# Attention and mixture-of-experts kernel: products copied out between two exponentials, one table step and three place matrices moved from GpSimd to ScalarE, and another order in the last slot

## The chip, the cores and the metric

One core of a Trainium2 chip runs one program. It has five engines with an instruction queue each, worked through in order: TensorE (PE, matrix products), VectorE (DVE), ScalarE (ACT), GpSimd (POOL) and SyncE (SP, here for DMA issue). The metric is the device time of one execution in microseconds (us); lower is better. Times of this kernel differ by about 0.2% between runs.

## The reference

```python
def _attn_ref(q, k, v):                     # each 8 x 8 heads x 576 x 64
    ...                                     # rotary embedding of q and k
    scores = scale * np.matmul(q_rot, k_rot.transpose(0, 1, 3, 2))
    scores = scores - np.max(scores, axis=-1, keepdims=True)
    attn = np.exp(scores)
    attn = attn / (np.sum(attn, axis=-1, keepdims=True) + 1e-09)
    return np.matmul(attn, v).astype(np.float32)

def _moe_ref(x, w_gate, w_output_gate, w1, w2):   # x: 4608 x 512, 8 experts, 1024 wide
    logits = x @ w_gate
    e_idx = np.argmax(logits, axis=1)
    ...                                     # gate_w: softmax at e_idx; eom: sigmoid(x @ w_output_gate)
    for e in range(E):
        mask = e_idx == e
        h = np.maximum(x[mask] @ w1[e], 0.0)
        out[mask] = gate_w[mask, None] * eom[mask, e, None] * (h @ w2[e])
```

Attention runs first; its output, with heads and channels brought together, is the x of the experts. Each token goes to one expert.

## The kernel before

The program has two stages. **Attention** takes 32 pairs of heads (8 batches of 4 pairs), one after another, up to about 482 us. A pair has nine units of 128 rows of scores (the two heads' last 64 rows share unit 4), taken in five steps: units 0 and 1, 2 and 3, 4, 5 and 6, 7 and 8. **The experts** take 23 slots of up to 256 tokens of one expert, and in them TensorE sets the pace.

A pair goes through the engines so: TensorE computes a unit's scores into the tile `sc` (L504, twelve matmuls for two units); VectorE copies them to `pm` and takes the row maximum in one instruction (L513, "peak"); ScalarE does the exponential in place with the row sum (L520, "exp"); VectorE transposes `pm` into `pt` (L528 two units in one instruction, L525 one unit). One pair later TensorE multiplies `pt` with the values into `acc` (L550, in four pieces av0 to av3). Then `den0` adds 1e-9 to the row sums (L531, POOL), `den1` takes reciprocals (L534, DVE), `den2` copies one column (L537, ACT), `evict` copies `acc` to `ac` in three instructions (L557 to L559, ACT), `back` turns `ac` round into `acc` again (L565, PE), and `divide` writes the pair's output to `xb` (L577, DVE). Only one `acc` exists, so a pair's first product waits for the `divide` of the pair before it. `pm` has two buffers of two units each (PM).

Ahead of that, POOL rotates a coming pair's q and k (two multiplications L455, one addition L459 and one subtraction L468); ScalarE rounds the result to the type that TensorE takes (`kq`, L465) and copies the last rows' block (`bd`, L475).

After the fourth pair of a batch, `place` finds each token's expert and its row in the experts' lists, spread over the pairs of the next batch as steps s0 to s22: small POOL operations, and at the end five "ones" matrices `ro` (L728 and L729, ACT) and five place matrices `pl` (L738, POOL: where a column's number equals `lo`, the token's number `tok`, else 0), which TensorE multiplies into a list (s20, L746). That list is copied as `lc` (L752, ACT) and added to `lists` (L755, POOL). For the last batch this work is VectorE's and comes behind attention.

The order is written by hand. EVENTS names for each part of a pair an offset in units and a sub-step k; `at` files it there, and `step` issues for each group of units scores, peaks, transposes (TURNS says which units are turned at which step; step 0's entry belongs to the pair before), exps, and then all parts that are filed there, by group and k. ROWS and PLACES do the same for `ro` and `pl`. A framework adds the semaphores; nothing is reordered.

In the experts, a slot's `second` (L1163) does the second layer: four parts of 12 matmuls, the two halves `py_0` and `py_1` of the slot (128 tokens each) taking turns. `store` scales the halves (L1172 on ACT, L1174 on DVE) and scatters the rows to the output by an indirect DMA from POOL (L1175). A second scatter to `out` waits until the first has landed. After the last slot the program ends with branch and closing instructions (L1237, L1273).

Of the kernel before, what the change touches and what calls it, by code (L numbers as in the profile page):

```python
# [47 lines left out]
    ("av0", 12, 1), ("av1", 13, 1), ("av2", 15, 1), ("av3", 17, 1),  # L48
    ("den0", 10, 2), ("den1", 15, 2), ("den2", 16, 2), ("evict", 17, 2), ("newxb", 18, 1), ("back", 19, 1), ("divide", 19, 2),
# [215 lines left out]
class Attention:  # L265
# [89 lines left out]
    def step(self, g):  # L355
# [3 lines left out]
        if g < G:  # L359
# [7 lines left out]
            for u in units:  # L367
                pr.peak(u)
            self.turns(g)
            for u in units:  # L370
                pr.exp(u)
# [7 lines left out]
    def turns(self, g):  # L379
        n, i = divmod(g, 9)  # L380
        n -= i == 0
        if 0 <= n < len(self.pairs):
            self.pairs[n].turn(TURNS.get(i, ()))


class Pair:
# [135 lines left out]
    def turn(self, units):  # L522

        if len(units) == 1:
            self.nc.vector.transpose(out=self.pt[:, 4, :], in_=self.pc[units[0]])  # L525
        elif units:
            c = self.STEPS[units[0]][0]
            self.nc.vector.transpose(out=self.pt[:, c:c + 6:5, :], in_=self.pc[units])  # L528

    def den0(self):  # L530
        self.nc.gpsimd.tensor_scalar(self.rz, self.z, 1e-9, None, op0=ALU.add)  # L531
# [55 lines left out]
def place(tc, pools, pairs, b, NT, cc, trib, oneb, cnt, xbs, xd, row, lists, later):  # L587
# [13 lines left out]

    CE = [P, NCH, E]
# [109 lines left out]
    def s17():  # L712
# [7 lines left out]
        V.tensor_scalar(new("tok", [P, NCH]), cc(C_TOK), number(NT, b), None, op0=ALU.add)  # L720
# [27 lines left out]
    def s21():  # L748
        if last:
            nc.vector.tensor_tensor(out=lists, in0=T["ls"], in1=lists, op=ALU.add)  # L750
# [3 lines left out]
    def s22():  # L754
        nc.gpsimd.tensor_tensor(out=lists, in0=T["lc"], in1=lists, op=ALU.add)  # L755
# [32 lines left out]
class Moe:  # L788
# [363 lines left out]
    def second(self, s, j):  # L1152
        hth, htl = self.ht[s]
        K = self.todo[s][0]
        if j == 0:
# [8 lines left out]
        self.wp.pop(8 * s + 4 + j)  # L1164

    def store(self, s):
        nc = self.nc
        py, gs = self.pys.pop(s), self.gss.pop(s)
        y = self.buf("y", s, 2, 0, [P, 2, DM], F32, f"y{s}{self.nm}")
        for h in range(self.todo[s][0]):  # L1170
            if h == 0:
                nc.scalar.activation(y[:, 0, :], py[0], AF.Copy, scale=gs[:, 0:1])  # L1172
            else:
                nc.vector.tensor_scalar(y[:, 1, :], py[1], gs[:, 1:2], None, op0=ALU.mult)  # L1174
            nc.gpsimd.indirect_dma_start(  # L1175
# [113 lines left out]
```

## Time and profile before

| | us |
|---|---|
| median of three runs (lowest, highest) | 986.09 (985.11, 987.06) |
| the profiled execution | 985.03 |
| its span in the trace | 983.3 |
| attention, from start to the last divide | about 482 |
| transition to the experts | about 482 to 505 |
| experts, to TensorE's last matmul | to 968.4 |
| from there to the end | 14.9 |

The profiled execution took 985.03 us, its span is 983.3 us and 1.73 us lie around it. All rows are of that execution. In an answer of the trace a row begins with its start and its duration in us; "[x <-y]" means that the engine sat idle for x before it and that y ended the wait. In a table by lines, "x27 | 25.9, 960" is 27 instructions, 25.9 us busy and 960 ns for one. A duration runs longer than the distance from one start to the next where instructions overlap; for sums the distance between starts counts.

### The profile page before, as it was taken

Reading aid. Unit: us, or ns where it says so; the run is one execution under the profiler, and the core shown is the slowest. Engines: PE = TensorE matmul, PEld = TensorE weight load, DVE = VectorE, ACT = ScalarE, POOL = GpSimd, SP = SyncE. Lnnn points to the kernel's source line nnn. Section 1 sums busy time; section 2 is a strip of 40 time slices with the busy share of each in tenths; the row PEclk is TensorE's granted clock in tenths of the full one; section 3 lists DMA queues with packets and bytes.
Section 4 is the critical chain, followed back from the end, with each engine's and each line's share of the span. In section 5 each row is a group of like instructions: output and inputs, shape, how many; then the busy total and the mean of one; then the engine's idle time right before and its main releaser. Section 6 shows DMA issues by size and latency. Waiting matters only on the chain.

```text
span 983.3 us, 34130 instructions
## 1 busy us (share of the span) xinstructions
PE 898.3 (91%) x14413; PEld 780.4 (79%) x14413; DVE 759.7 (77%) x1322; ACT 629.1 (64%) x1278; POOL 563.4 (57%) x565
## 2 busy tenths in 40 slices
PE   4989888988989888988899999999999999999993
PEld 3777777767777777776688989999899999988993
DVE  6889998998999999998779766557766766667560
ACT  4676787876878778686654544457656656565460
POOL 5787899999999999998411212142504234050410
PEclk9999999999999999999999999999999999999997
DMA  6543454564555456353589867667876869678630
GB/s 231 195 174 129 187 222 144 201 239 145 202 203 190 165 195 236 130 212 110 185 309 286 315 221 237 222 221 266 305 239 241 302 195 336 203 248 291 216 107 20
DMA packets 57822, 208.39 MB, mean 212 GB/s; under 512 B 7946, under 2 KB 8252, under 8 KB 57664
## 3 DMA queue, kind: packets, MB, share of 16 engines
q1 hardware_dynamic: 49920, 183.78, 53.7%
q0 software_dynamic: 6464, 21.26, 5.8%
q8 instruction: 115, 1.88, 0.8%
q10 hardware_dynamic: 1280, 1.11, 0.3%
q14 instruction: 43, 0.35, 0.1%
HBM read 186.06 MB, written 22.43 MB: 212 GB/s over the span
## 4 chain that ended last, share of the span: by engine, by line
PE 57%; DVE 14%; POOL 14%; issue 5%; ACT 4%; DMA 4%; SPq 0%; POOLq 0%; DVEq 0%; ACTq 0%
PE py L1163 18%; PE ph L1121 17%; PE acc L550 8%; PE sc L504 7%; DVE pm L513 6%; POOL raw L455 5%; DVE pt L528 4%; POOL kq L468 4%; PE ph L1113 3%; POOL raw L459 2%; ACT pm L520 2%; DVE xb L577 2%; PE mtp L1086 2%; DVE wl L1080 1%; POOL pl L738 1%
## 5 line engine op out<-in xcount | busy, mean ns | idle before, releaser
L520 ACT ACTIVATE pm<-pm,m 128x576 f32<-128x576 f32 x288 | 221.5, 770 | 96.2 <-DVE pm L513 94.2
L1080 DVE TENSOR_TENSOR wl<-wr,wh 128x1024 fp32r<-128x1024 f32 x172 | 216.0, 1270 | 37.5 <-ACT wh L1078 35.6
L513 DVE TENSOR_SCALAR_CACHE_REDUCE pm<-sc 128x576 f32<-128x576 f32 x288 | 207.7, 754 | 33.2 <-PE sc L504 26.1
L550 PE MATMUL acc<-pt,v 32*64 32x160 f32 (+1 forms) x9216 | 197.6, 295 | 18.6 <-DVE xb L577 6.9
L1163 PE MATMUL py<-wh,ht 128*128 128x512 f32 x640 | 213.1, 399 | 0.0
L1121 PE MATMUL ph<-xt,wh 128*128 128x256 f32 x1088 | 195.5, 282 | 0.5 <-DVE xt L1102 0.5
L550 PEld LDWEIGHTS acc<-pt,v 32*64 32x64 f32 x9216 | 157.4, 131 | 44.4 <-issue 22.0
L1078 ACT CAST wh<-wr 128x1024 fp32r<-128x1024 f32 x184 | 187.9, 1049 | 0.0
L528 DVE STREAM_TRANSPOSE pt<-pm 128x1152 f32<-128x1152 f32 x128 | 175.7, 1373 | 0.0
L1121 PEld LDWEIGHTS ph<-xt,wh 128*128 128x128 f32 x1088 | 167.8, 188 | 3.5 <-DVE xt L1102 2.2
L504 PE MATMUL sc<-kq 64*128 64x288 f32 x1536 | 149.8, 318 | 18.1 <-ACT kq L465 9.4
L455 POOL TENSOR_TENSOR raw<-raw,rt 128x1152 f32<-128x1152 f32 x62 | 164.3, 2651 | 0.6
L504 PEld LDWEIGHTS sc<-kq 64*128 64x128 f32 x1536 | 115.1, 190 | 47.7 <-issue 16.2
L1121 PE MATMUL ph<-xt,wl 128*128 128x256 f32 x544 | 152.8, 281 | 0.0
L1163 PEld LDWEIGHTS py<-wh,ht 128*128 128x128 f32 x640 | 120.3, 188 | 24.1
L1163 PE MATMUL py<-wl,ht 128*128 128x512 f32 x320 | 125.0, 391 | 0.0
L1175 POOL DMA_INDIRECT out<-y,2idx x24 | 28.2, 1174 | 168.3 <-ACT y L1172 122.8
L1137 ACT ACTIVATE ht<-ph 128x512 fp32r<-128x512 f32 x68 | 40.7, 598 | 108.7 <-PE ph L1121 108.7
L1121 PEld LDWEIGHTS ph<-xt,wl 128*128 128x128 f32 x544 | 102.5, 188 | 0.2
L1138 DVE SCALAR_TENSOR_TENSOR ht<-ph,ht 128x512 fp32r<-128x512 f32 x68 | 47.0, 691 | 69.1 <-ACT ht L1137 69.1
L468 POOL TENSOR_TENSOR kq<-raw,kq 128x1152 fp32r<-128x1152 f32 (+1 forms) x33 | 82.7, 2507 | 9.4 <-ACT kq L465 9.4
L459 POOL TENSOR_TENSOR raw<-raw 128x1152 f32<-128x1152 f32 (+1 forms) x33 | 82.5, 2499 | 1.8
(247 smaller groups left out, 1055.5 us busy)
## 6 DMA issues: line engine op xcount, KB each, us to landing
wr<-in_w SPq DMA_DIRECT2D x184, 512.0 KB, 4.9
raw<-in_qk SPq DMA_DIRECT2D x64, 576.0 KB, 4.9
v<-in_v SPq DMA_DIRECT2D x64, 576.0 KB, 6.8
xd<-xb SPq DMA_DIRECT2D x16, 640.0 KB, 4.4
xd<-xb SPq DMA_DIRECT2D x8, 160.0 KB, 5.0
rt<-in_rope ACTq DMA_DIRECT2D x1, 576.0 KB, 5.5
xg<-xd,2idx POOLq DMA_INDIRECT x24, 6.9
out<-y,2idx POOLq DMA_INDIRECT x24, 4.5
```

The costliest lines, as they stand in the source:

```text
L455: self.eng(eng).tensor_tensor(out=rv, in0=rv, in1=rt, op=ALU.mult)
L459: self.eng(eng).tensor_tensor(out=r, in0=r, in1=self.sides(self.raw, t, 1, x), op=ALU.add)
L468: self.eng(eng).tensor_tensor(out=self.sides(self.kq, t, 0, x), in0=self.sides(self.raw, t, 0, x), in1=self.sides(self.kq.bitcast(F32), t, ...
L504: self.nc.tensor.matmul(self.ps[i][:, a, :HS], st, self.kq[r, mov, x], start=(n == 0), stop=(n == 2))
L513: self.nc.vector.tensor_scalar(self.halves(i), self.ps[i][:, :, :HS], 1.0, FAR, op0=ALU.mult, op1=ALU.min, accum_out=self.m[i])
L520: self.nc.scalar.activation(self.pc[i], self.pc[i], AF.Exp, bias=self.m[i], scale=-1.0, accum_out=self.z[:, zi:zi + 1])
L528: self.nc.vector.transpose(out=self.pt[:, c:c + 6:5, :], in_=self.pc[units])
L550: nc.tensor.matmul(self.acc[h * D:h * D + D, a, o:o + 32 * n], self.v[r, h, j, :], self.pt[r, u:u + n, 32 * j:32 * j + 32], start=(j == 0) ...
L1078: self.nc.scalar.copy(wh, r)
L1080: eng.tensor_tensor(out=wl, in0=r, in1=wh.bitcast(F32), op=ALU.subtract)
L1121: nc.tensor.matmul(ph[:, f, :], st[:, dc, fs], mv[:, dc, :], start=(n == 0), stop=(n == 11))
L1163: self.nc.tensor.matmul(py[h], st[:, f, hs], mv, start=(f == 0 and n == 0), stop=(f == 7 and n == 2))
```

## The change

1. `av1` to `av3` are filed under sub-step 0, and `step` now issues sub-step 0 ahead of the exps and sub-step 1 between the first and the second exp of a group. `den2` is filed one unit earlier, `evict` in sub-step 1 of the group of units 7 and 8. So ScalarE copies the products out between exp 7 and exp 8.
2. The transpose of units 7 and 8 is split: unit 7 is turned right behind units 5 and 6, unit 8 alone one step later.
3. `den0` becomes a ScalarE Copy with a bias.
4. For all batches but the last, the first three of a batch's five place matrices (TURNED = 3) become two ScalarE activations each: a Square of `lo` minus the row number, then a Relu with `tok` as bias and minus `tok` (`tik`, one new small POOL operation) as scale, each through a pointer to one value per partition. Signs are arranged so that `tok` is not negative.
5. In the last slot, `close` does all 24 matmuls of `py_0` first, scales and scatters it, and then `py_1`. Both scalings are on ScalarE, and the second scatter no longer waits for the first one's landing. A `drain` is issued to POOL's queue at the first step of the last slot; it stands there right ahead of the slot's two scatters.

```diff
     ("lasts", 1, 2), ("loadv0", 5, 2), ("loadv1", 7, 2),
-    ("av0", 12, 1), ("av1", 13, 1), ("av2", 15, 1), ("av3", 17, 1),
-    ("den0", 10, 2), ("den1", 15, 2), ("den2", 16, 2), ("evict", 17, 2), ("newxb", 18, 1), ("back", 19, 1), ("divide", 19, 2),
+    ("av0", 12, 1), ("av1", 13, 0), ("av2", 14, 0), ("av3", 16, 0),
+    ("den0", 10, 2), ("den1", 15, 2), ("den2", 15, 3), ("evict", 16, 1), ("newxb", 18, 1), ("back", 19, 1), ("divide", 19, 2),
...
+TURNED = 3
...
-TURNS = {0: (7, 8), 2: (0, 1), 4: (2, 3), 5: (4,), 7: (5, 6)}
+TURNS = {0: ((8,),), 2: ((0, 1),), 4: ((2, 3),), 5: ((4,),), 7: ((5, 6), (7,))}
...
                 pr.peak(u)
+            self.now(g, 0)
+            for n, u in enumerate(units):
+                if n == 1:
+                    self.now(g, 1)
+                pr.exp(u)
             self.turns(g)
-            for u in units:
-                pr.exp(u)
             group = tuple(g + k for k in range(len(units)))
...
-            self.pairs[n].turn(TURNS.get(i, ()))
+            for units in TURNS.get(i, ()):
+                self.pairs[n].turn(units)
...
+        c, h = self.STEPS[units[0]] or (4, 0)
         if len(units) == 1:
-            self.nc.vector.transpose(out=self.pt[:, 4, :], in_=self.pc[units[0]])
-        elif units:
-            c = self.STEPS[units[0]][0]
+            self.nc.vector.transpose(out=self.pt[:, c + 5 * h, :], in_=self.pc[units[0]])
+        else:
             self.nc.vector.transpose(out=self.pt[:, c:c + 6:5, :], in_=self.pc[units])
...
     def den0(self):
-        self.nc.gpsimd.tensor_scalar(self.rz, self.z, 1e-9, None, op0=ALU.add)
+        self.nc.scalar.activation(self.rz, self.z, AF.Copy, bias=1e-9)
...
+    sign = -1.0 if number(NT, b) < 0 else 1.0
...
-        V.tensor_scalar(new("tok", [P, NCH]), cc(C_TOK), number(NT, b), None, op0=ALU.add)
+        V.tensor_scalar(new("tok", [P, NCH]), cc(C_TOK), sign, sign * number(NT, b), op0=ALU.mult, op1=ALU.add)
+        if not last:
+            V.tensor_scalar(new("tik", [P, NCH]), T["tok"], -1.0, None, op0=ALU.mult)
...
+        if not last and c < TURNED:
+            nc.scalar.activation(T["pl"][:, c, :], row[:, 0:P], AF.Square, bias=T["lo"][:, c:c + 1], scale=-1.0)
+            nc.scalar.activation(T["pl"][:, c, :], T["pl"].bitcast(F32)[:, c, :], AF.Relu, bias=T["tok"][:, c:c + 1], scale=T["tik"][:, c:c + 1])
+            return
         V.tensor_scalar(T["pl"][:, c, :], row[:, 0:P], T["lo"][:, c:c + 1], T["tok"][:, c:c + 1], op0=ALU.is_equal,
                                 op1=ALU.mult)
...
-        nc.gpsimd.tensor_tensor(out=lists, in0=T["lc"], in1=lists, op=ALU.add)
+        nc.gpsimd.tensor_tensor(out=lists, in0=lists, in1=T["lc"], op=ALU.subtract if sign < 0 else ALU.add)
...
+    def second(self, s, j, halves=None):
...
-            for h in range(K):
+            for h in range(K) if halves is None else halves:
                 hs = slice(h * P, h * P + P)
                 for n, (st, mv) in enumerate(((hth, wh), (hth, wl), (htl, wh))):
                     self.nc.tensor.matmul(py[h], st[:, f, hs], mv, start=(f == 0 and n == 0), stop=(f == 7 and n == 2))
...
+    def close(self, s):
+
+        before = None
+        for h in range(self.todo[s][0]):
+            for j in range(4):
+                self.second(s, j, (h,))
+            if h == 0:
+                py, gs, y = self.pys[s], self.gss.pop(s), self.buf("y", s, 2, 0, [P, 2, DM], F32, f"y{s}{self.nm}")
+            self.nc.scalar.activation(y[:, h, :], py[h], AF.Copy, scale=gs[:, h:h + 1])
+            st = self.scatter(s, h, y)
+            if before is not None:
+                self.tc.declare_no_dep(st.ins, before.ins, reason="a token is in one half of one slot: the rows are others")
+            before = st
+        self.pys.pop(s)
+        for j in range(4):
+            self.wp.pop(8 * s + 4 + j)
...
-            else:
+            elif not last:
                 self.second(s, j - 4)
...
-                self.store(s)
+                self.close(s) if last else self.store(s)
             if j == 6:
                 self.gather(s + 2)
+            if j == 0 and last:
+                self.nc.gpsimd.drain()
```

**VectorE, end of a pair.** `pm_7` holds units 7 and 8, `pm_0` units 0 and 1 of the next pair; `pm_5` and `pm_0` share a buffer. Before:

```order
L513 TENSOR_SCALAR pm_7_2471,m_7_2486<-sc_7_2472 128x576
L513 TENSOR_SCALAR pm_7_2471,m_8_2488<-sc_8_2473 128x576
L528 STREAM_TRANSPOSE pt_2254<-pm_5_2403 128x2x576
L513 TENSOR_SCALAR pm_0_2541,m_0_2556<-sc_0_2542 128x576
L513 TENSOR_SCALAR pm_0_2541,m_1_2558<-sc_1_2543 128x576
L528 STREAM_TRANSPOSE pt_2254<-pm_7_2471 128x2x576
L577 TENSOR_TENSOR xb_1686<-acc_2317,rz_116 128x5x160
L513 TENSOR_SCALAR pm_2_2578,m_2_2593<-sc_2_2579 128x576
```

After:

```order
L518 TENSOR_SCALAR pm_7_2485,m_7_2500<-sc_7_2486 128x576
L518 TENSOR_SCALAR pm_7_2485,m_8_2502<-sc_8_2487 128x576
L533 STREAM_TRANSPOSE pt_2264<-pm_5_2415 128x2x576
L531 STREAM_TRANSPOSE pt_2264<-pm_7_2485 128x576
L518 TENSOR_SCALAR pm_0_2555,m_0_2570<-sc_0_2556 128x576
L518 TENSOR_SCALAR pm_0_2555,m_1_2572<-sc_1_2557 128x576
L531 STREAM_TRANSPOSE pt_2264<-pm_7_2485 128x576
L582 TENSOR_TENSOR xb_1690<-acc_2328,rz_116 128x5x160
L518 TENSOR_SCALAR pm_2_2592,m_2_2607<-sc_2_2593 128x576
```

The transpose of unit 7 moved ahead of the next pair's first two peaks, and only unit 8's is left between them and the divide (L582, before L577).

**ScalarE, the same end of a pair, here in one that has `ro` matrices.** Before:

```order
L520 ACTIVATE pm_5_2403,z_111<-pm_5_2403,m_5_2418 128x576
L520 ACTIVATE pm_5_2403,z_111<-pm_5_2403,m_6_2420 128x576
L728 ACTIVATE ro_2291<-row,hr_2200 128x288
L729 ACTIVATE ro_2291<-ro_2291 128x288
L520 ACTIVATE pm_7_2471,z_111<-pm_7_2471,m_7_2486 128x576
L520 ACTIVATE pm_7_2471,z_111<-pm_7_2471,m_8_2488 128x576
L537 COPY rz_116<-rz_116 64x1
L557 COPY ac_117<-acc_2317 128x512
L558 COPY ac_117<-acc_2317 64x64
L559 COPY ac_117<-acc_2317 64x64
L520 ACTIVATE pm_0_2541,z_115<-pm_0_2541,m_0_2556 128x576
```

After:

```order
L525 ACTIVATE pm_5_2415,z_111<-pm_5_2415,m_5_2430 128x576
L525 ACTIVATE pm_5_2415,z_111<-pm_5_2415,m_6_2432 128x576
L736 ACTIVATE ro_2302<-row,hr_2252 128x288
L737 ACTIVATE ro_2302<-ro_2302 128x288
L747 ACTIVATE pl_2290<-row,lo_2253 128x128
L748 ACTIVATE pl_2290<-pl_2290,tok_2259,tik_2261 128x128
L542 COPY rz_116<-rz_116 64x1
L525 ACTIVATE pm_7_2485,z_111<-pm_7_2485,m_7_2500 128x576
L562 COPY ac_117<-acc_2328 128x512
L563 COPY ac_117<-acc_2328 64x64
L564 COPY ac_117<-acc_2328 64x64
L525 ACTIVATE pm_7_2485,z_111<-pm_7_2485,m_8_2502 128x576
```

`den2` and the three copies to `ac` moved ahead of exp 8 (the row with m_8), and two activations for one place matrix `pl` came in ahead of exp 7; two more pairs of them stand ahead of `bd` and behind the second `ro` of this pair.

**GpSimd, the first steps of the same pair.** Before:

```order
L720 TENSOR_SCALAR tok_2207<-ct 128x5
L459 TENSOR_TENSOR raw_1982<-raw_1982 128x2x576
L738 TENSOR_SCALAR pl_2280<-row,lo_2201,tok_2207 128x128
L531 TENSOR_SCALAR rz_116<-z_115 128x10
L455 TENSOR_TENSOR raw_2278<-raw_2278,rt 128x1152
L668 COPY xb_578<-eg_2019 128x2
L468 TENSOR_TENSOR kq_2350<-raw_1982,kq_2350 128x2x576
L738 TENSOR_SCALAR pl_2280<-row,lo_2201,tok_2207 128x128 x2
L455 TENSOR_TENSOR raw_2278<-raw_2278,rt 128x1152
L459 TENSOR_TENSOR raw_2278<-raw_2278 128x2x576
L738 TENSOR_SCALAR pl_2280<-row,lo_2201,tok_2207 128x128
```

After:

```order
L726 TENSOR_SCALAR tok_2259<-ct 128x5
L728 TENSOR_SCALAR tik_2261<-tok_2259 128x5
L464 TENSOR_TENSOR raw_1987<-raw_1987 128x2x576
L460 TENSOR_TENSOR raw_2286<-raw_2286,rt 128x1152
L674 COPY xb_578<-eg_2026 128x2
L473 TENSOR_TENSOR kq_2361<-raw_1987,kq_2361 128x2x576
L460 TENSOR_TENSOR raw_2286<-raw_2286,rt 128x1152
L464 TENSOR_TENSOR raw_2286<-raw_2286 128x2x576
L750 TENSOR_SCALAR pl_2290<-row,lo_2253,tok_2259 128x128
```

Three of the place matrices and the two additions to `rz` are gone from the rows, and `tik` (L728) came in.

## Rows read from the trace of the kernel before

**Rows 1.** Windows: length, busy us of each engine, TensorE clock, DMA share, GB/s.
```profile
60.00:440.00 380.00, 337.39 (x9338) 281.18 (x9335) 354.99 (x698) 293.33 (x741) 356.66 (x367) 1.00 0.53 190
74.15:88.03 13.88, 12.62 (x356) 10.53 (x356) 13.28 (x27) 10.00 (x26) 10.01 (x5) 1.00 0.49 178
130.10:143.98 13.88, 12.56 (x356) 10.48 (x354) 13.28 (x27) 12.68 (x32) 13.64 (x10) 1.00 0.60 226
505.00:968.00 463.00, 461.87 (x2996) 416.93 (x2995) 312.17 (x453) 257.82 (x355) 126.05 (x88) 1.00 0.72 246
```

**Rows 2.** Groups by line on VectorE, 60 to 440 us; behind the bar busy, mean, idle.
```profile
L513 DVE TENSOR_SCALAR_CACHE_REDUCE pm<-sc 128x576 f32<-128x576 f32 x237 | 170.9, 753 | 21.0 <-PE sc L504 14.3
L528 DVE STREAM_TRANSPOSE pt<-pm 128x1152 f32<-128x1152 f32 x107 | 146.9, 1373 | 0.0
L577 DVE TENSOR_TENSOR xb<-acc,rz 128x800 f32<-128x800 f32 x27 | 25.9, 960 | 2.4 <-ACT bd L475 1.0 <-DMA raw<-in_qk 0.9 <-PE acc L746 0.5
...
L627 DVE TENSOR_REDUCE fx<-sc 128x5 f32<-128x40 f32 x6 | 1.1, 183 | 1.6 <-POOL sc L624 1.5
```

**Rows 3.** Timeline of VectorE, the end of the pair whose divide is at 143.98.
```profile
137.36 0.77 DVE L525 STREAM_TRANSPOSE pt<-pm 128x576 f32<-128x576 f32 x1
138.06 0.17 DVE L534 RECIPROCAL rz<-rz 128x10 f32<-128x10 f32 x1
...
139.82 1.37 DVE L528 STREAM_TRANSPOSE pt<-pm 128x1152 f32<-128x1152 f32 x1
141.32 0.76 DVE L513 TENSOR_SCALAR_CACHE_REDUCE pm<-sc 128x576 f32<-128x576 f32 x1
...
142.68 1.37 DVE L528 STREAM_TRANSPOSE pt<-pm 128x1152 f32<-128x1152 f32 x1
143.98 0.95 DVE L577 TENSOR_TENSOR xb<-acc,rz 128x800 f32<-128x800 f32 x1
```

**Rows 4.** Timeline of ScalarE at the same place.
```profile
139.26 0.78 ACT L520 ACTIVATE pm<-pm,m 128x576 f32<-128x576 f32 x1
...
140.04 0.76 ACT L520 ACTIVATE pm<-pm,m 128x576 f32<-128x576 f32 x1
...
141.12 0.59 ACT L557 COPY ac<-acc 128x512 f32<-128x512 f32 x1
...
141.82 0.21 ACT L559 COPY ac<-acc 64x64 f32<-64x64 f32 x1
```

**Rows 5.** Waits of TensorE, 60 to 440 us: in total, times, longest.
```profile
PE acc L565 <- ACT ac L559: 26.1, 26, 1.5
```

**Rows 6.** Groups by line on ScalarE, 60 to 440 us.
```profile
L728 ACT ACTIVATE ro<-row,hr 128x288 fp32r<-128x288 bf16 x29 | 15.3, 526 | 0.3
...
L729 ACT ACTIVATE ro<-ro 128x288 fp32r<-128x288 f32 x29 | 12.9, 444 | 0.9
```

**Rows 7.** Groups by line on GpSimd, 60 to 440 us.
```profile
L738 POOL TENSOR_SCALAR pl<-row,lo,tok 128x128 fp32r<-128x128 bf16 x29 | 23.4, 807 | 0.0
```

**Rows 8.** Waits of VectorE, 434 to 490 us (the last batch and the transition).
```profile
DVE fx L627 <- POOL sc L624: 1.5, 1, 1.5
DVE xb L577 <- PE acc L565: 1.3, 1, 1.3
DVE mx L614 <- POOL lgs L611: 1.3, 1, 1.3
DVE xb L577 <- PE acc L746: 1.1, 1, 1.1
```

**Rows 9.** Timeline of GpSimd from 962 us.
```profile
968.69 0.98 POOL L1175 DMA_INDIRECT out<-y,2idx  x1 [19.61 <-ACT y L1172]
972.62 0.98 POOL L1175 DMA_INDIRECT out<-y,2idx  x1 [2.94 <-DMA out<-y,2idx]
```

**Rows 10.** Timeline of VectorE from 966 us.
```profile
968.42 0.75 DVE L1174 TENSOR_SCALAR y<-py,gs 128x512 f32<-128x512 f32 x1 [9.63 <-PE py L1163]
```

**Rows 11.** The program's last line: sequencer instructions, ns min/median/max, first and last start.
```profile
L1273 POOLq DRAIN  x3: 46/254/6773, 975.2 to 983.0; - x3
```

More of the change, by code (lines that the diff above doesn't have):

```diff
@@ L749, in s21 @@
         if last:
-            nc.vector.tensor_tensor(out=lists, in0=T["ls"], in1=lists, op=ALU.add)
+            nc.vector.tensor_tensor(out=lists, in0=lists, in1=T["ls"], op=ALU.subtract if sign < 0 else ALU.add)
             return
@@ L1150, in across @@
         self.nc.vector.tensor_tensor(out=htl[:, js, 0:P], in0=tp[:, 0:2, :], in1=hth.bitcast(F32)[:, js, 0:P], op=ALU.subtract)
-    def second(self, s, j):
+    def second(self, s, j, halves=None):
         hth, htl = self.ht[s]
         K = self.todo[s][0]
-        if j == 0:
+        if s not in self.pys:
             self.pys[s] = [self.pm.tile([P, DM], F32, tag=f"py{h}", name=f"py{s}_{h}{self.nm}") for h in range(K)]
@@ L1163, in second, with scatter @@
                     self.nc.tensor.matmul(py[h], st[:, f, hs], mv, start=(f == 0 and n == 0), stop=(f == 7 and n == 2))
-        self.wp.pop(8 * s + 4 + j)
+        if halves is None:
+            self.wp.pop(8 * s + 4 + j)
+    def scatter(self, s, h, y):
+        return self.nc.gpsimd.indirect_dma_start(
+            out=self.out, out_offset=bass.IndirectOffsetOnAxis(ap=self.ids(s, h), axis=0),
+            in_=y[:, h, :], in_offset=None, bounds_check=self.NT - 1, oob_is_err=False)
     def store(self, s):
-        nc = self.nc
         py, gs = self.pys.pop(s), self.gss.pop(s)
@@ L1171, in store @@
             if h == 0:
-                nc.scalar.activation(y[:, 0, :], py[0], AF.Copy, scale=gs[:, 0:1])
+                self.nc.scalar.activation(y[:, 0, :], py[0], AF.Copy, scale=gs[:, 0:1])
             else:
-                nc.vector.tensor_scalar(y[:, 1, :], py[1], gs[:, 1:2], None, op0=ALU.mult)
-            nc.gpsimd.indirect_dma_start(
-                out=self.out, out_offset=bass.IndirectOffsetOnAxis(ap=self.ids(s, h), axis=0),
-                in_=y[:, h, :], in_offset=None, bounds_check=self.NT - 1, oob_is_err=False)
+                self.nc.vector.tensor_scalar(y[:, 1, :], py[1], gs[:, 1:2], None, op0=ALU.mult)
+            self.scatter(s, h, y)
+    def close(self, s):
[12 more added lines that the diff above has]
+        for j in range(4):
+            self.wp.pop(8 * s + 4 + j)
     LOADS, SPLITS, LEAD = 8, 9, 6
@@ L1200, in more, with slot @@
             self.split(u)
-    def slot(self, s, left, per=2):
+    def slot(self, s, left, per=2, last=False):
         for j in range(8):
@@ L1229, in run @@
         for s in range(N):
-            self.slot(s, left)
+            self.slot(s, left, last=s == N - 1)
         while left:
```

## Prediction

> **What bounds the kernel now.** I read the windows by stage first, then the groups and waits of the busiest engine in each stage, then the timelines at the places that the change touches, and the end of the program last.
>
> In the experts TensorE is busy 461.87 of 463 us [rows 1]: nothing else counts there, and what attention gains or loses passes on one to one, since the experts start when the last batch's output is there. In attention, over 380 us, POOL is busy 356.66, VectorE 354.99 and ScalarE 293.33 [rows 1]. VectorE is the one that waits for next to nothing: 25.0 us of idle time, in which the peaks' 14.3 behind TensorE's scores are the largest part, 2.4 stand ahead of the divide and 1.6 ahead of L627 [rows 2]. POOL's high share is work for later pairs, and of VectorE's waits only L627's 1.5 name it. So a pair lasts as long as VectorE's list: 13.88 us in a pair without extras [rows 1]. At most the 25 us could be won in this stretch by whatever the other engines do.
>
> What differs between pairs is ScalarE's load: 10.00 us of 13.88 in a pair without `ro` matrices, 12.68 in one with three [rows 1]. There ScalarE has 1.20 us left.
>
> The end: the second scatter waits 2.94 us for the first to land [rows 9], and of POOL's three closing DRAINs the longest takes 6.77 us, the first starting at 975.2 [rows 11]; the span ends at 983.3.
>
> **The split transpose.** In the pair of [rows 3] the double transposes start at 139.82 and 142.68. Behind the second the divide starts 1.30 later; behind the first the next peak starts 1.50 later, and that peak writes the buffer that this transpose reads. A single one takes 0.70 to the next start (137.36 to 138.06), a peak 0.68 (two from 141.32 to 142.68). Before, this end is 1.50 + 1.36 + 1.30 = 4.16 from 139.82; after it is 1.30 (double) + 0.70 (unit 7) + 1.36 (two peaks) + 0.70 (unit 8) = 4.06. I take the 1.50 to become 1.30, because another transpose stands behind it and the buffer is free by the time of the peak. That is -0.10 a pair, over 31 pairs **-3.1 us**. If the 0.20 is no matter of the buffer, the split costs +0.10 a pair, +3.1; that is the upper end.
>
> **The copies between the exps.** Before, exp 7 and exp 8 start at 139.26 and 140.04, the three copies go from 141.12 to 142.03 [rows 4], and TensorE waits for them about 1.0 us in every pair (26.1 us in 26 waits [rows 5]). After, the copies begin where exp 8 stood, about 140.1, so `back` comes about 1.0 earlier. In an ordinary pair the divide does not wait for it, and nothing is won. Where a batch's list product stands between `back` and the divide, it does: VectorE's 2.4 us ahead of the divide [rows 2] go, **-2.4**. Exp 8 ends about 1.0 us later, near 141.95; its transpose is due at 139.82 + 1.30 + 0.70 + 1.36 = 143.18, so some 1.2 us of cover are left. If that goes, each 0.1 us costs 3.1 us in all. Earlier scores might also take some of the peaks' 14.3 us; they recur at other places than `back`, so I take nothing, with 5 us as the lower end.
>
> **Relief of POOL.** It loses three `pl` a batch at 0.81 each [rows 7] and the small `den0`, and gets a small `tik`. L627's 1.5 us for POOL [rows 2] go, **-1.5**. In the last batch and the transition VectorE's waits for POOL and for `acc` are 1.5, 1.3, 1.1, and 1.3 for TensorE's `back` [rows 8]; the first two go by the relief, the last two by the earlier copies: **-5.2**. Half of that is the cautious end. `den0` on ScalarE stands ahead of `bd`; between the exp at 140.04 and the copy at 141.12 lie 1.08 us, less the exp's own 0.78 [rows 4] leaves 0.30 for a readout and `den2`, so a small copy costs between 0 and 0.30; I take 0.15. With 3.88 us idle in an ordinary pair that is free.
>
> **The place matrices on ScalarE.** A Square with one pointer over 288 columns takes 526 ns, a Relu with immediate values 444 ns [rows 6]; an exp over 576 takes 0.77 [rows 4], so a column costs (770 - 526) / 288 = 0.85 ns, and 128 columns come to 0.39 and 0.31 us. The new Relu has two pointers; one pointer is worth 526 - 444 = 82 ns, so it takes 0.47. Together 0.86, and as starts lie a little closer than durations I take 0.82 a matrix. Without any price for pointers it is 0.62, the lower end. In a pair with three of them ScalarE gets 3 x 0.82 + 0.15 = 2.6 us on 1.20 us of room [rows 1], 1.4 too much. Laid out by hand behind the peaks, exp 7 ends 1.27 us after its transpose is due; the next pair has fewer matrices and recovers. Six batches meet this inside attention: 6 x 1.27 = **+7.6** (at 0.62 it is 0.65 each, +3.9). The seventh batch's matrices fall in the transition, where ScalarE waits anyway: 0, up to +2.
>
> The Trainium skill, "ScalarE: Activation LUTs", section "What ACT_TABLE_LOAD costs", gives 186 ns and 0.833 ns a column, about 93 ns more for each pointer operand, and an overlap of about 93 ns between neighbours. The 526 and 444 ns of [rows 6] agree with it within 20 ns; as an estimate from that page a matrix would take 0.68, the loss would be 5 us, and the total 2.6 us lower than mine.
>
> **The last slot.** Before, the first scatter starts at 968.69 and the second at 972.62 [rows 9]. After, the first half is scattered some 5 us earlier, hidden behind the second half's matmuls; the second half's scaling starts where it started on VectorE, 968.42 [rows 10], takes about 0.7 on ScalarE, and its scatter can start 0.27 later, as the first one now does, at about 969.4: 972.62 - 969.4 = **-3.2**. The cost of halves for TensorE is nothing: the same 48 matmuls, and all weights are there.
>
> **The drain.** POOL is idle for 19.6 us ahead of the last scatters [rows 9], so an early drain is covered, even at 6.8 us. The question is what the last DRAIN then costs. The three of [rows 11] take 6773, 254 and 46 ns, all at the same place in the program; the two later ones, behind an emptied queue, are short. I take it that the long one works off what POOL's queue has gathered over the program, and that only two scatters are left for it: 6.77 falls to about 0.25, **-6.5**. The other end is 0.
>
> **Sum.** Attention: -3.1 - 2.4 - 1.5 - 5.2 + 7.6 = -4.6. End: -3.2 - 6.5 = -9.7. Against the profiled execution's 985.03 that gives 970.7. That execution stands 1.06 us below the median of the runs, so the forecast is 971.7.
>
> **Rivals.**
> A. The last DRAIN stays long: a price of the last scatters or of the closing itself, not of the queue's history. For it: no row shows a drain behind scatters that is short, since the two short ones come behind the long one. Against it: the long one goes on until 982.0, some 9 us after the last scatter's start, where the first scatter was down 3 us after its own (968.69, and its waiter goes on at 972.62). Time: 971.7 + 6.5 = 978.2. The Trainium skill, "GPSIMD Engine Reference", section "Instruction dispatch", says that the first call into freshly loaded code costs about 6 us and shows as no instruction; by that, scatters behind the early drain could make the last one pay once more, which is this rival. No row here shows such a load.
>
> B. ScalarE's room in the place pairs does not help, since it lies in pieces ahead of other exps: all 2.6 us are lost, 6 x (2.6 - 1.27) = +8.0, 979.7. For it: in that pair ScalarE's idle time is only 1.20 us. Against: late exps catch up within the pair.
>
> C, on the other side: the copies hold up exp 8. It decides in every pair once exp 8 ends more than 1.2 us later than worked out, because the copies must wait for the last product or because ScalarE runs behind. At 0.55 us beyond that, 31 x 0.55 = +17: 988.7, slower than before; with A, 0.35 us beyond is enough. For it: the copies now stand ahead of an exp in an in-order queue, and the waits of [rows 5] show how near product, copy and `back` lie. Against it: 1.2 us of cover.
>
> **How the numbers follow.** Forecast 0.58 (966 to 976 for itself), A 0.25, B 0.10, C 0.07. Lower end: 971.7 less 3.7 (matrices at 0.62) and 5 (scores) is 963. Upper end: A with half of the waits of the last batch back, 981. A measurement of this kernel can tell about 0.2%, 2 us, from no change. The forecast, A and most of B are faster: 0.88; within 0.2%: 0.05, from B and C with parts of A; slower 0.07.
>
> **What would show it.** Right: the last DRAIN under 1 us, and a second scatter that starts about 1 us after TensorE's last matmul; the divides at batch ends without wait; ordinary pairs of about 13.8 us; pairs with three matrices about 1.2 us longer than now, with a transpose waiting for exp 7. Wrong: a DRAIN of 6 to 7 us at the end (A), peaks or transposes waiting more than 2 us in each place pair (B), a wait of unit 8's transpose for ScalarE in every pair (C).

## The result, and the profile after

| | before | after |
|---|---|---|
| median of four runs, us | 985.63 (985.11 to 987.06) | 973.61 (973.14 to 974.04) |
| ratio, 95% interval | | 0.9876 (0.9858 to 0.9893) |
| span of the profiled execution | 983.3 | 971.9 |

The forecast was 971.7 in a range of 963 to 981. The median fell by 12.0 us, well clear of the runs' spread; the span fell by 11.4 us, 2.9 less than the 14.3 of the sum. Cut at the divides, at TensorE's last matmul and at the end, the two traces differ so:

| stretch | before | after | difference | worked out |
|---|---|---|---|---|
| start to the second divide | 60.27 | 58.52 | -1.75 | +0.6 with the next line |
| second to 28th divide | 374.31 | 376.96 | +2.65 | |
| 28th to 31st divide | 48.11 | 42.16 | -5.95 | -5.2 with the next line |
| 31st divide to the experts' fifth ReLU | 37.88 | 38.52 | +0.64 | |
| fifth to last ReLU of the experts (L1137, after L1149) | 436.90 | 439.19 | +2.29 | 0 |
| last ReLU to TensorE's end | 10.92 | 10.95 | +0.03 | 0 |
| TensorE's end to the end of the span | 14.87 | 5.61 | -9.26 | -9.7 |

("Worked out" shares out the prediction's terms by where they fall.) Attention and the end came out near their sums (attention by luck in part, as the waits below show); the line that the sum did not have is the experts' pace.

The windows of the kernel after, to be held against [rows 1] (columns as there): the whole stretch, an ordinary pair, a full pair (three `pl` and three `ro`), the experts.

```profile
60.00:440.00 380.00, 345.65 (x9311) 286.32 (x9293) 352.37 (x722) 309.03 (x798) 337.88 (x331) 0.99 0.53 189
115.41:129.29 13.88, 12.80 (x356) 10.54 (x354) 13.39 (x29) 10.41 (x29) 10.39 (x15) 1.00 0.33 117
129.29:145.70 16.41, 13.67 (x349) 11.31 (x347) 13.52 (x27) 15.97 (x44) 14.28 (x8) 0.90 0.70 259
505.00:960.00 455.00, 454.08 (x2949) 410.32 (x2948) 307.72 (x445) 255.08 (x350) 128.96 (x88) 1.00 0.73 246
```

ScalarE is busy 15.97 us in the pair with the place matrices, where it had 12.68 in [rows 1], and that pair takes 16.41 instead of 13.88. Of the six full pairs three take 16.4 us and three 15.1. Ordinary pairs are not all alike, so the one at 115.41 has to be held against the same pair before, which took 13.98 us. It is 0.10 shorter, as the split was to give:

```profile
116.12:130.10 13.98, 12.55 (x358) 10.52 (x358) 13.44 (x28) 10.20 (x28) 10.76 (x17) 1.00 0.35 121
```

VectorE's waits in the same stretch, against [rows 2]:

```profile
DVE pm L518 <- PE sc L509: 12.1, 42, 1.8
DVE pt L531 <- ACT pm L525: 7.1, 6, 1.2
DVE xb L582 <- PE acc L570: 3.7, 3, 1.2
```

L627's and the divide's old waits are gone. In their place stand six waits of a transpose for an exp, 1.2 us each, and three of a divide for `back`, 1.2 us each. VectorE's timeline shows both in the pair that ends at 145.70:

```profile
139.12 1.37 DVE L533 STREAM_TRANSPOSE pt<-pm 128x1152 f32<-128x1152 f32 x1
141.68 0.78 DVE L531 STREAM_TRANSPOSE pt<-pm 128x576 f32<-128x576 f32 x1 [1.18 <-ACT pm L525]
142.38 0.72 DVE L518 TENSOR_SCALAR_CACHE_REDUCE pm<-sc 128x576 f32<-128x576 f32 x1
...
143.71 0.78 DVE L531 STREAM_TRANSPOSE pt<-pm 128x576 f32<-128x576 f32 x1
145.70 0.99 DVE L582 TENSOR_TENSOR xb<-acc,rz 128x800 f32<-128x800 f32 x1 [1.22 <-PE acc L570]
```

Unit 7's transpose (141.68) could have started at 140.42, 1.30 behind the double one, and waits for exp 7. All six waits for an exp are of unit 7. The end of the program, against [rows 9] and [rows 11], is GpSimd's timeline, then the early DRAIN, the closing ones, and the instruction ahead of them (ns min/median/max):

```profile
961.81 0.98 POOL L1180 DMA_INDIRECT out<-y,2idx  x1 [15.09 <-ACT y L1202]
967.30 0.98 POOL L1180 DMA_INDIRECT out<-y,2idx  x1 [4.51 <-ACTq L1271]
```

```profile
L1254 POOLq DRAIN  x1: 8895/8895/8895, 944.5 to 944.5; - x1
```

```profile
L1307 POOLq DRAIN  x3: 46/112/2273, 968.3 to 971.6; - x3
```

```profile
L1271 POOLq INC_SWDGE_SEM  x1: 246/246/246, 968.0 to 968.0; - x1
```

The early DRAIN takes 8.9 us while GpSimd has nothing else to do; the closing one takes 2.3 instead of 6.8. Before, the other instruction took 1.8:

```profile
L1237 POOLq INC_SWDGE_SEM  x1: 1839/1839/1839, 973.3 to 973.3; - x1
```

### The profile page after: what moved, and what is told of

Read it like the earlier page. It is cut to its first block, busy times and chain, and to the rows that moved or that the text cites. A ratio compares the mean times of both kernels' runs of the same rounds, so it can differ in the third digit from the quotient of the medians.

```text
span 971.9 us, 34146 instructions
## 1 busy us (share of the span) xinstructions
PE 910.4 (94%) x14413; PEld 787.9 (81%) x14413; DVE 759.1 (78%) x1353; ACT 650.2 (67%) x1353; POOL 542.2 (56%) x519
## 4 chain that ended last, share of the span: by engine, by line
PE 43%; issue 4%; DVE 3%; ACT 2%; POOL 1%; DMA 1%; POOLq 0%; ACTq 0%; DVEq 0%
PE py L1175 19%; PE ph L1133 18%; PE ph L1125 3%; PE mtp L1098 1%; DVE wl L1092 1%; DMA out<-y,2idx 1%; ACT wh L1090 1%; PE acc L555 1%; PE htp L1160 0%; PE sc L509 0%; POOL kq L473 0%; POOL wl L1092 0%; POOLq L1254 0%; DVE ht L1150 0%; POOL out L1180 0%
## 5 line engine op out<-in xcount | busy, mean ns | idle before, releaser
L509 PE MATMUL sc<-kq 64*128 64x288 f32 x1536 | 156.6, 319 | 18.1 <-ACT kq L470 9.5
L509 PEld LDWEIGHTS sc<-kq 64*128 64x128 f32 x1536 | 118.7, 191 | 51.5 <-DVE pm L518 19.8
L533 DVE STREAM_TRANSPOSE pt<-pm 128x1152 f32<-128x1152 f32 x96 | 131.8, 1373 | 0.1
L1149 ACT ACTIVATE ht<-ph 128x512 fp32r<-128x512 f32 x68 | 40.6, 597 | 109.0 <-PE ph L1133 106.6
L473 POOL TENSOR_TENSOR kq<-raw,kq 128x1152 fp32r<-128x1152 f32 (+1 forms) x33 | 82.5, 2500 | 10.9 <-ACT kq L470 10.7
```

Source lines behind the costliest of these rows:

```text
L473: self.eng(eng).tensor_tensor(out=self.sides(self.kq, t, 0, x), in0=self.sides(self.raw, t, 0, x), in1=self.sides(self.kq.bitcast(F32), t, ...
L509: self.nc.tensor.matmul(self.ps[i][:, a, :HS], st, self.kq[r, mov, x], start=(n == 0), stop=(n == 2))
```

## The experiments

`b_` kernels are built on the kernel before, all others on the one after. Spans are of the profiled executions. The same attention code differs from run to run by up to about 1.2 us between the second and the 28th divide (375.9 to 377.1 in four kernels that agree there), in single pairs by up to 1.3 (batch ends, and which full pairs meet the half clock, below), so single microseconds of attention are read from waits and not from spans.

### The end: three places for the drain

`b_drain` puts the drain alone into the kernel before; `a_nodrain` takes it out of the kernel after; `a_mid` has it in slot 11 of 23.

```diff
+            if j == 0 and last:          # b_drain, on before
+                self.nc.gpsimd.drain()
...
-            if j == 0 and last:          # a_nodrain, on after
-                self.nc.gpsimd.drain()
...
-            if j == 0 and last:          # a_mid, on after
+            if j == 0 and s == 11:
                 self.nc.gpsimd.drain()
```

> The kernel before, with nothing changed but a drain in GpSimd's queue at the first step of the last slot. Theory (the long closing DRAIN is a price of what the queue did earlier, and it can be paid while GpSimd is idle): from the last scatter's start to the end of the span 10.7 us before become about 4.6, so the time falls from 985.6 to about 979.5; the early DRAIN takes several us in the idle time of 19 us. Rival (the tail became short in the changed kernel because the scatters no longer wait for each other): the closing DRAIN stays near 6.8 us and the time at 985.6. The run also shows the experts' pace of an otherwise unchanged kernel: if the experts' 437 us between the fifth and the last slot's first ReLU are now near 439, the changed kernel's slower experts are no effect of the change.

> The changed kernel without its early drain. Theory: the closing DRAIN is again 6 to 7 us and the instruction ahead of it 1.8 us, time 973.6 + 6.1 = 979.7. Rival (the halves made the tail short): 973.6, closing DRAIN near 2.3 us.

> The changed kernel with its early drain at the first step of slot 11 in place of the last slot. If the price grows with each transfer that GpSimd has issued since the last drain, about half of it is back at the end: closing DRAIN 2.3 + about 3, time about 976.5. If it is a price of the first drain after the start, the closing DRAIN stays near 2.3 us and the time at 973.6. If an early drain helps only when it stands close to the end, 979.7.

Medians: `b_drain` 981.06, ratio 0.9943 (0.9920 to 0.9965); `a_nodrain` 977.86, 4.2 above the kernel after where 6.1 were expected; `a_mid` 974.48. The closing rows of the three, in this order (that of the instruction ahead, then the DRAINs):

```profile
L1239 POOLq INC_SWDGE_SEM  x1: 246/246/246, 975.3 to 975.3; - x1
```

```profile
L1275 POOLq DRAIN  x3: 52/173/1761, 975.6 to 978.9; - x3
```

```profile
L1269 POOLq INC_SWDGE_SEM  x1: 1839/1839/1839, 966.6 to 966.6; - x1
```

```profile
L1305 POOLq DRAIN  x3: 46/107/6773, 968.5 to 975.8; - x3
```

```profile
L1271 POOLq INC_SWDGE_SEM  x1: 939/939/939, 966.8 to 966.8; - x1
```

```profile
L1307 POOLq DRAIN  x3: 46/107/3076, 967.8 to 971.5; - x3
```

The drain alone makes the closing short, with or without halves: the rival that the halves did it falls. The price grows with the transfers that GpSimd has issued since the last drain. All 82 indirect transfers stand ahead of the end without a drain, 37 behind the drain of slot 11, two behind that of the last slot, and the first instruction takes 1839, 939 and 246 ns: (1839 - 246) / 80 = 19.9 and (939 - 246) / 35 = 19.8 ns a transfer. The long DRAIN follows the count as well: 6773 / 82 = 82.6 and 3076 / 37 = 83.1 ns a transfer. Behind two transfers that would be under 0.2 us, and what is seen there is the last scatter: in the kernel after it lands at 970.40 and the DRAIN ends at 970.53, and in `b_drain`, `a_spread` and `x1` too the DRAIN (1.8 to 2.2 us) ends 0.13 to 0.14 us behind the landing. It fits that `a_mid`'s 3.1 us are less than the 2.3 + 3 that were expected, as if landing and price ran side by side.

From the last scatter's start to the end of the span it is 10.2 us without a drain, 5.6 with the one in slot 11 and 4.6 with the one in the last slot. So the queue's history is what is paid for; an early drain pays it in idle time. Time since the last drain grows along with the count; for the count speaks that `before` and `a_nodrain` have the same 1839 and 6773 ns, though from the first transfer to the closing they take 505.7 and 504.1 us. What it is in the transfers that costs, their number or what they move, no run separates. The early DRAIN itself is not in proportion to the count (8.0 us in slot 11 behind 45 transfers, 8.9 in the last behind 80); both start with a scatter just issued, and I leave that open.

Of the tail's 14.87 us the halves alone take away 3.7 (`a_nodrain` has 11.17) and the drain alone 6.3 (`b_drain` has 8.53), both together 9.3. `a_nodrain`'s tail is 5.6 us longer than that of the kernel after; only 4.2 of it show in the spans, because its TensorE happened to be done 1.4 us earlier.

### Which place matrices, and where

`a_spread` has three a batch on ScalarE as well, but others, so that one falls into the full pair and two into the next:

```diff
-TURNED = 3
+TURNED = (0, 3, 4)
...
-        if not last and c < TURNED:
+        if not last and c in TURNED:
```

> The changed kernel with other place matrices on ScalarE: the first, fourth and fifth of a batch in place of the first three. The same number on ScalarE, but only one of them in the pair with three ro matrices and two in the next one. Theory (ScalarE is late in that pair alone, 1.18 us in each of six, and TensorE's wait that follows costs another 1.22 us in three of them by a halved clock): both go, -7.1 - 3.7 = about 962.8, TensorE's granted clock 1.00 there. Rival (the three matrices cost their time on ScalarE wherever they stand): 973.6, with the waits in the next pair. Rival (GpSimd, with two matrices in the first pair, is late there): 968 or more, with waits for it.

Median 966.39, ratio 0.9774 (0.9719 to 0.9828), span 964.2. Windows of the full pair and the next one, and VectorE's waits:

```profile
129.10:142.91 13.81, 12.54 (x355) 10.51 (x353) 13.32 (x28) 13.46 (x35) 13.69 (x9) 1.00 0.64 219
142.91:158.12 15.21, 13.39 (x360) 11.07 (x359) 13.47 (x31) 13.71 (x36) 14.58 (x13) 1.00 0.74 271
```

```profile
DVE pm L518 <- PE sc L509: 14.1, 46, 1.5
```

Both new waits are gone, and the full pair takes 13.81 us with ScalarE busy for 13.46 of them. From the second to the 28th divide it is 366.08 instead of 376.96 us, -10.9, as the two waits' sum of 10.8 said. Only 7.7 of it reach the span, so that 962.8 was missed: from the 28th to the 31st divide it is 45.44 and not 42.16. GpSimd has two more matrices just ahead of the last batch's table steps there, and L633 waits 1.4 us for it at 440 us; `x1`, below, takes one of them away and has 42.21.

The 1.2 us waits of the divide in the kernel after are TensorE's clock. Windows of the kernel after around two of the six places (the column behind POOL is the granted clock):

```profile
140.50:142.60 2.10, 0.00 (x0) 0.00 (x0) 0.92 (x2) 1.99 (x7) 2.10 (x1) 0.96 0.88 314
142.60:145.70 3.10, 3.07 (x12) 2.74 (x12) 1.89 (x5) 3.06 (x10) 1.06 (x2) 0.50 0.93 369
199.10:201.20 2.10, 0.00 (x0) 0.00 (x0) 0.94 (x2) 1.99 (x8) 2.10 (x1) 1.00 0.83 255
201.20:203.00 1.80, 1.79 (x13) 1.62 (x14) 1.80 (x6) 1.80 (x5) 1.03 (x2) 1.00 1.02 392
```

```profile
142.63 3.03 PE L570 MATMUL acc<-ii,ac 128*128 128x160 f32 x10 [2.23 <-ACT ac L564]
201.21 1.63 PE L570 MATMUL acc<-ii,ac 128*128 128x160 f32 x10 [2.23 <-ACT ac L564]
374.55 3.03 PE L570 MATMUL acc<-ii,ac 128*128 128x160 f32 x10 [1.26 <-ACT ac L564]
```

In all six places `back` waits for the copies behind the late exp 7, 2.2 us in four of them and 1.2 to 1.3 in two, where TensorE had also stood idle shortly before. In three the granted clock behind it is 0.50, 1.2 instead of 2.4 GHz, and the ten matmuls of `back` take 3.03 us (waits of 2.23, 2.23 and 1.26); in the other three it stays at 1.00, and they take 1.63 (waits of 2.23, 1.22 and 2.22). `a_nodrain`, `a_mid` and `a_align`, with the same attention code, have the half clock at other places of the six. So the length of this wait does not decide it, nor the place, and the rows do not tell what does.

### The experts' pace

The kernel after, `a_nodrain`, `a_mid` and `a_spread` all had 439.2 us between the fifth and the last ReLU, `b_drain` 437.2. The granted clock is 1.00 in all of them. The two buffers of the new small tile `tik` move tiles behind them in the on-chip memory by 64 bytes. In the built program six of the nine buffers of the experts' split weights `wh` and `wl` start at a multiple of 128 bytes before the change; `tik` moves these six, while the other three stay 64 bytes past a multiple, so that none starts at one after the change. `a_align` makes `tik` larger, so that the shift is 128 bytes:

```diff
-            V.tensor_scalar(new("tik", [P, NCH]), T["tok"], -1.0, None, op0=ALU.mult)
+            V.tensor_scalar(new("tik", [P, 16])[:, 0:NCH], T["tok"], -1.0, None, op0=ALU.mult)
```

> The changed kernel with one edit: the new small tile tik takes 64 bytes a buffer in place of 32, so that all tiles behind it lie 128 and not 64 bytes further than in the kernel before, and six of the nine buffers of the experts' split weights start at a multiple of 128 again, as before the change. Theory (the experts run 2.2 us slower since the change because their weights lie 64 bytes off): from the fifth to the last slot's ReLU 439.2 become 437.0 us, time 973.6 - 2.2 = 971.4. Rival (something else in the changed program, code or timing, slows TensorE there): 439.2 and 973.6.

Median 970.74, 2.9 below the kernel after. The first and the last of these ReLUs in ScalarE's timeline, before, after and in `a_align`:

```profile
520.57 0.60 ACT L1137 ACTIVATE ht<-ph 128x512 fp32r<-128x512 f32 x1 [3.25 <-PE ph L1121]
```

```profile
957.47 0.60 ACT L1137 ACTIVATE ht<-ph 128x512 fp32r<-128x512 f32 x1 [2.22 <-PE ph L1121]
```

```profile
516.16 0.60 ACT L1149 ACTIVATE ht<-ph 128x512 fp32r<-128x512 f32 x1 [3.31 <-PE ph L1133]
```

```profile
955.35 0.60 ACT L1149 ACTIVATE ht<-ph 128x512 fp32r<-128x512 f32 x1 [2.28 <-PE ph L1133]
```

```profile
516.28 0.60 ACT L1149 ACTIVATE ht<-ph 128x512 fp32r<-128x512 f32 x1 [3.25 <-PE ph L1133]
```

```profile
953.11 0.60 ACT L1149 ACTIVATE ht<-ph 128x512 fp32r<-128x512 f32 x1 [2.23 <-PE ph L1133]
```

436.90, 439.19 and 436.83 us: the shift is the cause of the 2.3 us. But `a_align` does not bring back the old pace of every part. Over the same three stretches, TensorE's busy time (first column behind the length) in the first layer, tile `ph`, and in the second, tile `py`:

```profile
520.57:957.47 436.90, 220.13 (x1800) 216.31 (x1799) 43.52 (x63) 46.96 (x87) 1.00 0.73 248
516.16:955.35 439.19, 221.48 (x1800) 217.79 (x1799) 43.48 (x63) 46.87 (x87) 1.00 0.73 246
516.28:953.11 436.83, 218.34 (x1800) 214.80 (x1799) 43.55 (x63) 46.88 (x88) 1.00 0.73 248
```

```profile
520.57:957.47 436.90, 211.71 (x865) 158.31 (x866) 11.91 (x16) 14.48 (x21) 1.00 0.73 248
516.16:955.35 439.19, 212.93 (x865) 158.51 (x866) 11.86 (x16) 14.46 (x21) 1.00 0.73 246
516.28:953.11 436.83, 213.72 (x865) 158.34 (x866) 11.93 (x16) 14.47 (x21) 1.00 0.73 248
```

In `a_align` the first layer is 1.8 us faster than before the change and the second 2.0 us slower, so its equal total is partly chance. That a multiple of 128 is what is wanted, I tested in `x2` (on `x1`, below), where all weight buffers and the experts' other large tiles start at one:

```diff
-            self.gss[s] = self.buf("gs", s, 2, 2, [P, 2], F32, f"gs{s}{self.nm}")
+            self.gss[s] = self.buf("gs", s, 2, 2, [P, 24 if s % 2 else 32], F32, f"gs{s}{self.nm}")[:, 0:2]
```

> The kernel x1 with the small tile gs padded (24 and 32 values a partition in place of 2), so that all buffers of the experts' weights, xt and ht start at a multiple of 128 bytes. Theory (a weight buffer 64 bytes off slows the matmuls that read it; six of nine buffers were worth 2.36 us): the three that are still off give another 1.2 us, from the fifth to the last slot's ReLU 436.9 become 435.7, more if xt and ht count as well; time 961.8 - 1.2 = 960.6. Rival (only the six buffers matter, by where they lie to something else): 436.9 and 961.8.

It came out at 438.23 us (506.94 to 945.17) and 963.30 in the median, slower than `x1`'s 436.86 and 961.79. Both the theory and its rival missed. So the rule of 128 bytes falls; what stays is that where the tiles lie moves the experts' time by 0.3 to 0.5% with no instruction of the experts changed. It is the layout and not the single run: six kernels with the layout of the kernel after had 439.2 to 439.3 us, four with that of `a_align` 436.8 to 436.9, and two with that of `x2` 438.2 and 438.6. Which tiles must lie how to each other is open.

### The copies, the split and `den0`

Each is undone by itself, the first two in `a_spread`, where no exp is late.

```diff
-    ("av0", 12, 1), ("av1", 13, 0), ("av2", 14, 0), ("av3", 16, 0),          # s_oldev
+    ("av0", 12, 1), ("av1", 13, 1), ("av2", 15, 1), ("av3", 17, 1),
-    ... ("den2", 15, 3), ("evict", 16, 1), ...
+    ... ("den2", 16, 2), ("evict", 17, 2), ...
-TURNS = {0: ((8,),), ... 7: ((5, 6), (7,))}                                    # s_nosplit
+TURNS = {0: ((7, 8),), ... 7: ((5, 6),)}
```

> The kernel a_spread (first, fourth and fifth place matrix on ScalarE) with av1 to av3, den2 and the three copies at their old places behind exp 8. The prediction's terms for the earlier copies: 2.4 us at the batch ends and 2.4 in the last batch and the transition; so the span of a_spread, 964.2, becomes about 969, with the divides waiting 0.5 us at each batch end. Rival (the copies ahead of exp 8 win nothing or hold up exp 8): 964 or below.

Median 973.29, span 970.2, +6.0 against `a_spread`. The divides' group by line:

```profile
L582 DVE TENSOR_TENSOR xb<-acc,rz 128x800 f32<-128x800 f32 x26 | 25.2, 971 | 4.2 <-ACT bd L480 3.7 <-PE acc L570 0.3
```

In `a_spread` this group's idle time is 0.1 us, here 4.2. The sum had 4.8 us for the copies.

> The kernel a_spread with units 7 and 8 turned in one transpose at the old place. Prediction's term: each pair 0.10 us longer, 964.2 + 3.1 = 967.3, with the peak of unit 0 starting 1.50 and not 1.30 us behind the transpose of units 5 and 6. Rival (the 0.20 us are no matter of the buffer, so the split costs 0.10 a pair): 961.1.

Median 969.58, span 968.9, +4.7. VectorE's timeline around one transpose of units 5 and 6 there, with its waits:

```profile
110.80 1.37 DVE L533 STREAM_TRANSPOSE pt<-pm 128x1152 f32<-128x1152 f32 x1
112.10 0.15 DVE L649 TENSOR_REDUCE og<-t 128x5 f32<-128x40 f32 x1
112.29 0.76 DVE L518 TENSOR_SCALAR_CACHE_REDUCE pm<-sc 128x576 f32<-128x576 f32 x1
...
114.95 0.95 DVE L582 TENSOR_TENSOR xb<-acc,rz 128x800 f32<-128x800 f32 x1
```

```profile
DVE pm L518 <- DVE pt L533: 2.4, 5, 0.5
```

The peak starts 1.49 us behind the transpose, even with a small reduction in between, and the view names the transpose as what it waits for: the 0.20 us are a matter of the buffer. The full pair takes 13.88 us with the double transpose and 13.81 with the split one, and most other pairs without a batch end differ by 0.06 to 0.12, so the split is worth nearly the 0.10 a pair that was worked out, some 3 us over 31 pairs. The rest of the 4.7 lies in single pairs (2.7 us longer in the last full pair, others at batch ends, 2.8 us shorter behind the 28th divide), which also vary by themselves.

> The kernel x1 with den0 on GpSimd again. The prediction priced the move at nothing on ScalarE and at a small relief of GpSimd, 0.26 us a pair: 961.8 to 963. Rival (den0 ahead of bd delays TensorE's next scores or the peaks): 961 or less.

```diff
-        self.nc.scalar.activation(self.rz, self.z, AF.Copy, bias=1e-9)
+        self.nc.gpsimd.tensor_scalar(self.rz, self.z, 1e-9, None, op0=ALU.add)
```

Median 963.52, 1.7 above `x1`; span 962.5, +2.5, but that is the slowest of its four runs, and the runs of the two kernels overlap (961.7 to 964.3 against 960.7 to 964.2). The peaks wait 17.7 us for scores instead of the 13.8 to 14.4 of `x1`, `x2` and `x3`. The direction is that of a relief of GpSimd; the size is not resolved.

### A version that beats both, and what GpSimd's relief is worth

`x1` is `a_spread` with the larger `tik`, and with the second place matrix on ScalarE as well in the batch ahead of the last two:

```diff
-        if not last and c in TURNED:
+        if not last and c in (TURNED + (1,) if early else TURNED):
```

> The kernel a_spread with tik at 64 bytes a buffer, and in the last but two batch also the second place matrix on ScalarE, so that GpSimd is not late when the last batch's table steps begin. Expected if both theories hold: a_spread's span 964.2, less 2.2 for the experts, less 2 to 3 of the 3.2 us that a_spread lost between the fourth-last and the last divides: about 959.5; median near 961. Rival (ScalarE is late again in that batch's pair): 961 to 962.5 of span.

Median 961.79, ratio to the kernel before 0.9756 (0.9727 to 0.9784), span 960.0: 11.8 us faster than the kernel after. From the 28th to the 31st divide it is 42.21, the experts take 436.86, and one wait of 0.4 us for an exp is left.

> The kernel x1 with no place matrix on ScalarE (all five of a batch on GpSimd, as before the change). Prediction's terms for GpSimd's relief: 1.5 us for L627 and 2.8 in the last batch, so 961.8 + 4 = about 966, with VectorE's waits for GpSimd back. Rival (the matrices were only a load for ScalarE, GpSimd has the room): 961.8 or less.

```diff
-        if not last and c in (TURNED + (1,) if early else TURNED):     # x_t0
+        if not last and c in ():
-        if not last and c in (TURNED + (1,) if early else TURNED):     # x3
+        if not last and not ahead and c in (TURNED + (1,) if early else TURNED):
```

Median 967.03, span 965.8, +5.8 against `x1`, of which 4.3 us lie between the 28th and the 31st divide. GpSimd is waited for again, in part ahead of the last batch:

```profile
DVE fx L633 <- POOL sc L630: 1.9, 4, 0.6
DVE mx L620 <- POOL lgs L617: 0.7, 1, 0.7
```

> The kernel x2 with all five place matrices of the last but one batch on GpSimd again. The transition then has no place matrix on ScalarE: the casts of xt no longer stand behind three of them (2.5 us of ScalarE ahead of the casts). Prediction's term said 0, up to +2 for them there. Theory (they cost about 1.2 us in the transition): 1.2 us less than x2, about 959.4. Rival (they fill time in which ScalarE waits, or GpSimd is late with its five): same as x2 or longer.

`ahead` is the last but one batch. Median 962.81, span 961.1 against `x2`'s 961.2. From the 31st divide to the experts' fifth ReLU it is 39.23 us against 38.53. So the matrices on ScalarE cost nothing in the transition, as the prediction put it; my theory of 1.2 us falls.

## Why the prediction came out as it did

**The drain and the last slot** were right in mechanism and nearly in size. The sum had -3.2 and -6.5, together -9.7, and the tail lost 9.3. Inside, the closing DRAIN keeps 2.3 us, not 0.25 and not "under 1 us", as the last scatter is still on its way when it starts (967.30 + 3.1 to land, the DRAIN ends at 968.3 + 2.3); in exchange the instruction ahead of it fell from 1.84 to 0.25, which I had left out. That the two nearly cancel is luck. Rival A, a price of the last scatters or of code that is loaded anew, is refuted by `a_mid`: two scatters behind a drain are cheap, 37 transfers cost more, 82 most. The trace thus gives no support to the Trainium skill's first-call cost ("GPSIMD Engine Reference", section "Instruction dispatch") as the cause of this DRAIN, since behind the same last scatters it took 2.3, 3.1 or 6.8 us.

**The place matrices.** 1.27 us for each of six pairs was worked out; unit 7's transpose starts 1.26 late (141.68 - 140.42) and waits 1.18 of it, for the reason given. A matrix takes by rows 386 + 495 ns in durations:

```profile
L748 ACT ACTIVATE pl<-pl,tok,tik 128x128 fp32r<-128x128 f32 x18 | 8.9, 495 | 1.0
L747 ACT ACTIVATE pl<-row,lo 128x128 fp32r<-128x128 bf16 x18 | 7.0, 386 | 0.0
```

Where several follow each other, their starts lie 0.42 and 0.40 us apart (478.75, 479.17, 479.57), which makes 0.82, the value taken. The page "ScalarE: Activation LUTs", section "What ACT_TABLE_LOAD costs", of the Trainium skill gives the durations within 20 ns. Its overlap of about 93 ns between neighbours shows behind the Relu (495 ns, the next start 0.40 us later) but not behind the Square (386 ns, 0.42), whose result the Relu reads; so 0.82 came out and not the 0.68 by the page. What the step lacked is what comes behind the late exp: the copies, then `back`, and TensorE's halved clock, 1.22 us in three of six pairs, 3.7 us that the sum had at nothing. I had followed VectorE and ScalarE, and looked for the wait's price only there.

**The copies, the relief and the split** won together more than their 12.2 us, which hid that omission: second to 28th divide, without the new waits of 7.1 + 3.7, is 8.2 us shorter, where -3.1, -2.4 and -1.5 had been put down for all of attention. That attention came out near its sum all the same is luck. Undone one by one they cost in the spans 6.0 (copies), 5.8 (place matrices), 4.7 (split) and 2.5 us (`den0`, priced at nothing and unsure). That is 19.0, more than the 13.9 us by which `x1` reaches the experts' fifth ReLU earlier than the kernel before, so they overlap. Of the first three 4.7, 2.2 and 2.6 us lie in the same six pairs at batch ends between the second and the 28th divide, of `den0` nothing.

**The experts** are the step that failed: "what attention gains or loses passes on one to one" took for granted that an unchanged stage keeps its time. A shift by 64 bytes, from a small tile of the other stage, cost 2.3 us there, most of the 2.9 by which the fall was overestimated. Rivals B and C did not happen: ScalarE lost 1.18 and not 2.6 us, and unit 8's transpose never waited.

## What to carry to other kernels

Where work is put on an engine with spare time on average, lay it out pair by pair: from the second to the 28th divide three matrices a batch cost 10.9 us more with three of them in the full pair than with one in it and two in the next, where ScalarE was never late. When a wait is priced, follow it to the engines behind it, the matmul clock included. After adding a tile, compare the time of stages that the edit does not touch; if they moved, try paddings and measure each, since no rule for a good one is known here.

## What the runs showed that I had not expected

- Shifting tiles by 64 bytes slowed TensorE's 437 us by 2.3 us, at a granted clock of 1.00 throughout; another layout, with all large tiles at multiples of 128 bytes, by 1.4. The rule is open.
- A wait of TensorE ahead of ten matmuls was followed by a granted clock of 0.50 in three places of six: behind 2.23, 2.23 and 1.26 us, and not behind 2.23, 1.22 and 2.22.
- GpSimd's closing instruction takes 19.8 to 19.9 ns for each indirect transfer since the last drain, and the DRAIN behind it about 83 ns for each (3.1 and 6.8 us behind 37 and 82); behind two it ends with the last scatter's landing, after 1.8 to 2.3 us.
